# Loading both MLP weights behind the last V of a decode attention kernel, with the MLP features interleaved over the partitions

## The chip, the cores and the metric

The kernel runs on one core of one Trainium2 chip. The metric is the device time of one launch in microseconds (us). Times are quoted as the median of the runs of one kernel.

## The reference

One query token, 32 heads, 32768 cached keys of 128 features each, then an MLP with 1376 hidden features.

```python
x = A_x                                             # [1, 1, 512], bf16
q = (layernorm(x) @ wq)                             # 32 heads x 128
scores = q . k_cache * 128 ** -0.5                  # k_cache [1, 32, 32768, 128]
o = softmax(scores) @ v_cache                       # v_cache of the same shape
h = x + o @ wo
z = layernorm(h) @ w1 + b1                          # w1 [512, 1376], b1 [1376]
act = z * tanh(softplus(z))                         # Mish
out = h + act @ w2                                  # w2 [1376, 512]
```

The two caches are 512 MiB of bf16. Everything else is small: w1 and w2 are 1.4 MB each, b1 is 2.75 KB.

Of the kernel before, what the change touches and what calls it, by code (L numbers as in the profile page):

```python
# [6 lines left out]
BF16 = mybir.dt.bfloat16  # L7
F32 = mybir.dt.float32
I32 = mybir.dt.int32
ALU = mybir.AluOpType  # L10
# [3 lines left out]
PE, ACT, DVE, POOL, SP = "pe", "act", "dve", "pool", "sp"  # L14
# [5 lines left out]
LAST_K = [128, 32, 32, 32, 32]  # L20
LAST_V = [32, 32, 32, 32, 64, 32, 16, 8, 8]

W1A = 5
W2A = 6

LAG = 8

# [2 lines left out]
PRIV = "_p"  # L30
# [172 lines left out]
def build_kernel(nc, A_x, A_k_cache, A_v_cache, A_wq, A_wo, B_w1, B_b1, B_w2, out, NE=4):  # L203
# [3 lines left out]
    H = HD // Dh  # L207
    Sk = A_k_cache.shape[2]
    F = B_w1.shape[1]
    assert D == 512  # L210
    KC = D // 128
    R = 8
    GH = Sk // (128 * R)
    NCOL = GH * R
    NK = H * GH
    FJ = (F + 127) // 128
    FLAST = F - (FJ - 1) * 128
    SC = 1.0 / math.sqrt(Dh)
    EPS = 1e-5
    NH0 = min(4, H)  # L220
# [4 lines left out]
    def sb(shape, dt, name):  # L225
        cm = nc.sbuf_tensor(name, shape, dt)
        t = cm.__enter__()
        allocs.append(cm)
        return t.ap()
# [10 lines left out]
    w1v = sb([128, KC, F], BF16, "w1_sb")  # L240
    w2v = sb([128, FJ, D], BF16, "w2_sb")
# [4 lines left out]
    identb = sb([128, 128], BF16, "identb")  # L246
# [10 lines left out]
    xcT = sb([128, KC], BF16, "xcT")  # L257
# [14 lines left out]
    yrs = sb([128, D], F32, "yrs")  # L272
    ycol = sb([128, KC], F32, "ycol")
    pscr = sb([1, 2], F32, "pscr")
    FP = FJ + FJ % 2
    b1r = sb([FP, 128], BF16, "b1r")
    b1T = sb([128, FJ], F32, "b1T")
    hs = sb([128, 8, FJ], F32, "hs")
    actT = sb([128, FJ], BF16, "actT")
# [2 lines left out]
    MEANX, SSQ, LNV, RSTD, EPSC, SSQ2, LNV2, RSTD2, MEANH = (lnb[:, 16 + i:17 + i] for i in range(9))  # L282

    S_b = ps([128, 512], "sps")
# [4 lines left out]
    T_b = [ps([128, R * 128], f"tps{i}", BF16) for i in range(2)]  # L289
# [6 lines left out]
    YC = yps[:, 0:KC]  # L296
    HROW = 128
    YM = yps[:, 256:257]
    pre = S_b

    loads = plan_loads(H, GH)
    kload, vload = {}, {}
# [5 lines left out]
    wqa = ring[:, wq_at:wq_at + KC * NH0 * Dh].rearrange("p (kc n) -> p kc n", kc=KC)  # L308
    wqb = ring[:, wq_at + KC * NH0 * Dh:wq_at + KC * HD].rearrange("p (kc n) -> p kc n", kc=KC) if H > NH0 else None
# [8 lines left out]

    sem = nc.alloc_semaphore
    sems = {e: sem(f"ev_{e}") for e in (PE, ACT, DVE, POOL, SP)}  # L320
    for c in (ACT + PRIV, DVE + "0" + PRIV, DVE + "1" + PRIV, PE + "0" + PRIV, PE + "1" + PRIV, "x", "xr", "b1", "wqa", "wqb", "wo", "w1a", "w1b", "w2a", "w2b", "w2c", "out"):
        sems[c] = sem(f"s_{c}")
    for ld in loads:
        if ld.chan not in sems:
# [16 lines left out]
    def program(S):  # L341
        t_ = nc.tensor
        a = nc.scalar
        v = nc.vector
        g_ = nc.gpsimd
        sp = nc.sync
# [12 lines left out]
        def load_weights(which):  # L359
            if which == "wqa":  # L360
                S.dma(SP, lambda: sp.dma_start(  # L361
                    wqa, A_wq[:, 0:NH0 * Dh].rearrange("(p kc) n -> p kc n", kc=KC)).then_inc(sems["wqa"], 16))
            elif which == "wqb" and H > NH0:
                S.dma(SP, lambda: sp.dma_start(
                    wqb, A_wq[:, NH0 * Dh:HD].rearrange("(p kc) n -> p kc n", kc=KC)).then_inc(sems["wqb"], 16))
            elif which == "wo":
                S.dma(SP, lambda: sp.dma_start(
                    wo_sb[:, :, :], A_wo.rearrange("(h k) n -> k h n", k=128)).then_inc(sems["wo"], 16))
            elif which == "w12":
                S.dma(SP, lambda: sp.dma_start(  # L370
                    w1v[:, :, 0:W1A * 128],
                    B_w1.rearrange("(kc p) f -> p kc f", p=128)[:, :, 0:W1A * 128]).then_inc(sems["w1a"], 16))
            elif which == "late":
                S.dma(SP, lambda: sp.dma_start(
                    w1v[:, :, W1A * 128:F],
                    B_w1.rearrange("(kc p) f -> p kc f", p=128)[:, :, W1A * 128:F]).then_inc(sems["w1b"], 16))
                for a_, b_, s_ in ((0, W2A, "w2a"), (W2A, FJ - 1, "w2b")):
                    S.dma(SP, lambda a_=a_, b_=b_, s_=s_: sp.dma_start(
                        w2v[:, a_:b_, :],
                        B_w2[a_ * 128:b_ * 128, :].rearrange("(j p) n -> p j n", p=128)).then_inc(sems[s_], 16))  # L380
                S.dma(SP, lambda: sp.dma_start(
                    w2v[0:FLAST, FJ - 1, :], B_w2[(FJ - 1) * 128:F, :]).then_inc(sems["w2c"], 16))

        S.dma(SP, lambda: sp.dma_start(xTb[:, :], A_x[0, 0, :].rearrange("(p kc) -> p kc", kc=KC)).then_inc(sems["x"], 16))
        order = [(ld.pos, ld) for ld in loads]
        order += [(-1.0, "wqa"), (GH - 0.5, "wqb"), (GH + 2 * LAG + 0.2, "wo"), (2 * GH + 2 * LAG + 0.2, "w12"), (1e9, "late")]
        for _, ld in sorted(order, key=lambda o: o[0]):
            if isinstance(ld, str):
                load_weights(ld)
            else:  # L390
                issue(ld)
        S.dma(SP, lambda: sp.dma_start(out[0, 0, :].rearrange("(g n) -> g n", g=4), outsb[0:128:32, :]).then_inc(sems["out"], 16),
              waits=["fin"])
        S.wait(SP, [("out", 16)])

        for x in range(NX):
# [5 lines left out]
        S.step(POOL, lambda: g_.memset(b1r[:, :], 0.0), name="b1z")  # L402
        S.dma(POOL, lambda: g_.dma_start(xrow[0:1, :], A_x[0:1, 0, :]).then_inc(sems["xr"], 16))
        S.dma(POOL, lambda: g_.dma_start(
            b1r[0:FJ - 1, :], B_b1[0:(FJ - 1) * 128].rearrange("(j m) -> j m", m=128)).then_inc(sems["b1"], 16), waits=["b1z"])
        S.dma(POOL, lambda: g_.dma_start(
            b1r[FJ - 1:FJ, 0:FLAST], B_b1[(FJ - 1) * 128:F].rearrange("(o m) -> o m", o=1)).then_inc(sems["b1"], 16))
        for k, done in (("k", f"kf{NK - GH - 1}"), ("v", f"pv{NK - 2 * GH - 1}")):
            for x in range(NX):
                S.dma(POOL, lambda x=x, k=k: g_.sem_inc(sems[f"{k}x{x}"], -16), waits=[done])  # L410
# [5 lines left out]
        S.step(DVE, lambda: v.memset(oneb[0:1, :], 1.0))  # L416
        S.step(DVE, lambda: v.memset(onesf[:, :], 1.0))
        S.step(DVE, lambda: v.memset(qT[:, H:H + 1], 0.0))
        S.step(DVE, lambda: v.memset(yps[:, :], 0.0), name="consts")


# [10 lines left out]
               name="ident", waits=["iota"])  # L432
# [213 lines left out]
        for t in range(GH):  # L646
            group(H, t)
            if t == LAG + 5:
                S.step(DVE, lambda: v.tensor_reduce(ysum[:, :], yrow[:, :], AXX, ALU.add), name="ysum",
                       waits=[f"yr{hl - 1}"])  # L650
                S.step(DVE, lambda: v.tensor_scalar_mul(MEANH, ysum[:, :], 1.0 / D), name="meanh", waits=["ysum"])

                for c in range(KC):
                    S.step(DVE, lambda c=c: v.tensor_tensor(
                        yrs[:, c * 128:(c + 1) * 128], yrow[:, c * 128:(c + 1) * 128], ident[:, :], ALU.mult),
                        waits=[f"yr{hl - 1}"], name=(f"yrs" if c == KC - 1 else None))
                S.step(DVE, lambda: v.tensor_reduce(
                    ycol[:, :], yrs[:, :].rearrange("p (c n) -> p c n", c=KC), AXX, ALU.add), name="ycol", waits=["yrs"])
            if t == LAG + 9:
                S.step(PE, lambda: t_.matmul(YC, ident[:, :], ycol[:, :], start=True, stop=False,  # L660
                                             skip_group_check=True), waits=["ycol"])
                S.step(PE, lambda: t_.matmul(T_b[0][:, 0:FP], b1r[:, :], identb[0:FP, 0:FP],
                                             is_transpose=True, start=True, stop=True),
                       name="b1t", waits=[("b1", 32), f"ev{NK - 2}", f"ev{NK - 1}"])
                S.step(DVE, lambda: v.tensor_copy(b1T[:, :], T_b[0][:, 0:FJ]), name="b1T", waits=["b1t"])
        for t in range(LAG):
            group(H + 1, t)

# [3 lines left out]
            name="oT", waits=[f"pv{NK - 1}", f"o1s{hl}"])  # L672
        y_cols(hl)
        for s in range(2):
            S.step(PE, lambda s=s: t_.matmul(
                YM, wbh[:, s:s + 1].to_broadcast([128, 128]), oT[:, :],
                start=False, stop=(s == 1), skip_group_check=True),
                waits=(["wbh"] if s == 0 else ()), name=("ym" if s == 1 else None))
        S.step(DVE, lambda: v.tensor_scalar(HC, YC, YM, MEANH, ALU.subtract, ALU.subtract),
               name="hc", waits=["ym"])  # L680
# [1 line left out]
        S.step(DVE, lambda: v.tensor_tensor(SQ, HC, HC, ALU.mult), name="sq2", waits=["hc"])  # L682
        S.step(DVE, lambda: v.tensor_reduce(SSQ2, SQ, AXX, ALU.add), name="ssq2", waits=["sq2"])
        S.step(DVE, lambda: v.tensor_copy(hcol[:, :], YC), name="hcol")
        for j in range(FJ):
            W = 128 if j < FJ - 1 else FLAST
            for kc in range(KC):
                S.step(PE, lambda j=j, W=W, kc=kc: t_.matmul(  # L688
                    pre[0:W, j:j + 1], w1v[:, kc, j * 128:j * 128 + W], xcT[:, kc:kc + 1],
                    start=(kc == 0), stop=(kc == KC - 1)),  # L690
                    name=("hid" if j == FJ - 1 and kc == KC - 1 else None),
                    waits=(["xcT", ("w1a", 16), f"exq{H - 1}"] if j == 0 and kc == 0
                           else [("w1b", 16)] if j == W1A and kc == 0 else ()))
            if j == FJ // 2:
                S.step(PE, lambda: t_.matmul(V_REG, onesm[:, :], SSQ2, start=True, stop=True), name="v2",
                       waits=["ssq2"])
        S.step(ACT, lambda: a.activation(LNV2, V_REG, ACTF.Ln, bias=EPSC), name="ln2", waits=["v2"])
        S.step(ACT, lambda: a.activation(RSTD2, LNV2, ACTF.Exp, scale=-0.5), name="rstd2", waits=["ln2"])
        for c in range(KC):
            S.step(PE, lambda c=c: t_.matmul(  # L700
                yps[32 * c:32 * c + 1, HROW:HROW + 128], hcol[:, c:c + 1], ident[:, :],
                start=False, stop=False, skip_group_check=True), waits=(["hcol"] if c == 0 else ()))
        z, zm, e, u, uz, den, rden = (hs[:, k, :] for k in range(7))
        S.step(DVE, lambda: v.scalar_tensor_tensor(z, pre[:, 0:FJ], RSTD2, b1T[:, :], ALU.mult, ALU.add),
               name="z", waits=["hid", "rstd2", "b1T"])
        S.step(DVE, lambda: v.tensor_scalar_min(zm, z, 30.0), name="zm", waits=["z"])
        S.step(ACT, lambda: a.activation(e, zm, ACTF.Exp), name="e", waits=["zm"])
# [5 lines left out]
        for j in range(FJ):  # L713
            W = 128 if j < FJ - 1 else FLAST
            waits = ["act"] if j == 0 else []
            if j in (0, W2A, FJ - 1):
                waits.append(({0: "w2a", W2A: "w2b"}.get(j, "w2c"), 16))
            for c in range(KC):
                S.step(PE, lambda j=j, W=W, c=c: t_.matmul(  # L719
                    yps[32 * c:32 * c + 1, HROW:HROW + 128], actT[0:W, j:j + 1], w2v[0:W, j, c * 128:(c + 1) * 128],  # L720
                    start=False, stop=(j == FJ - 1), skip_group_check=True),
# [47 lines left out]
```

## The kernel before: what the change touches

The SP queue issues all large loads in one order: wq, then K and V by pieces of 4 MB (the first K and the last V in smaller pieces), with wo and the first 640 of the 1376 columns of w1 slipped in early. The rest of w1, and w2, follow the last V.

```python
elif which == "w12":                      # early, in the third head
    w1v[:, :, 0:W1A * 128] <- B_w1.rearrange("(kc p) f -> p kc f", p=128)[:, :, 0:W1A * 128]   # 1280 B rows
elif which == "late":                     # after the last V
    w1v[:, :, W1A * 128:F] <- B_w1...[:, :, W1A * 128:F]                                       # 1472 B rows
    for a_, b_, s_ in ((0, W2A, "w2a"), (W2A, FJ - 1, "w2b")):
        w2v[:, a_:b_, :] <- B_w2[a_ * 128:b_ * 128, :].rearrange("(j p) n -> p j n", p=128)    # 1024 B rows
    w2v[0:FLAST, FJ - 1, :] <- B_w2[(FJ - 1) * 128:F, :]
# ... (each is one sp.dma_start with its own semaphore; condensed here)

# POOL's queue, at the start of the kernel: b1 as 10 rows of 256 B and a rest of 192 B
b1r[0:FJ - 1, :] <- B_b1[0:(FJ - 1) * 128].rearrange("(j m) -> j m", m=128)
b1r[FJ - 1:FJ, 0:FLAST] <- B_b1[(FJ - 1) * 128:F].rearrange("(o m) -> o m", o=1)
# ... (turned into columns b1T by one PE transpose while PE waits for V)

# the tail, after the last V: feature f = 128 j + p sits in partition p, column j
for j in range(FJ):                       # FJ = 11
    W = 128 if j < FJ - 1 else FLAST      # FLAST = 96
    for kc in range(KC):                  # KC = 4
        matmul(pre[0:W, j:j + 1], w1v[:, kc, j * 128:j * 128 + W], xcT[:, kc:kc + 1], ...)
# ... z, Mish -> actT
for j in range(FJ):
    for c in range(KC):
        matmul(yps[32 * c:32 * c + 1, HROW:HROW + 128], actT[0:W, j:j + 1], w2v[0:W, j, c * 128:(c + 1) * 128], ...)
```

(Assignments with an arrow stand for DMA starts.) In a w1 matmul the w1 block is the stationary operand, so it is what the weight load reads: the trace of the kernel before lists 44 weight loads of it, 40 of 128x128 and 4 of 128x96.

## Time and profile before

| | before |
|---|---|
| time, median of 6 runs | 1288.78 us (1288.39 to 1289.03) |
| span of the profiled run | 1286.6 us |
| DMA engines | 9 tenths or more busy in 39 of 40 slices, 426 GB/s |
| last V landed | 1277.35 us |
| last weights landed | 1283.31 us |
| output copy starts | 1284.18 us |

Two lines of the page of the kernel before; the digits are busy tenths in 40 equal slices of the span, and GB/s is what the DMA engines moved in each slice.

```profile
DMA  9999999999999999999999999999999999999998
GB/s 375 424 409 426 428 435 428 436 428 435 428 435 429 434 430 432 431 433 431 433 431 432 430 434 430 433 430 434 430 431 433 431 433 431 433 430 433 431 419 324
```

The load stream never drains (9 tenths in 39 of 40 slices): the kernel is DMA bound until the last V has landed at 1277.35. What follows is a tail of about 9 us in which a chain of small operations runs on three engines. The chain that ended last, in order of time (start us, length us, what), kernel before:

```profile
1257.87 19.49 DMA ring<-in_A_v_cache_dram
1277.35 0.04 issue
1277.40 0.41 PE ops L530 x8
...
1278.79 0.17 DVE xcT L681
1278.96 0.07 DVE lnb L682
1279.03 0.92 PE sps L688 x24
1279.95 0.43 PE hlp L695 x2
1280.38 0.76 PE sps L688 x20
...
1282.55 0.18 DVE actT L712
1282.74 0.04 issue
1282.78 1.37 PE yps L719 x44
1284.15 0.02 issue
1284.18 0.29 DVE outsb L723
```

The 44 w1 matmuls are the two rows with `sps L688`: 24 take 0.92 us, 38 ns each. The 44 w2 matmuls are `yps L719`. No DMA appears after 1277.35, so the tail is bound by computing; the weights arrive just in time. Their loads, from the page's list of DMA issues (KB each, median us from issue to landing); the 640 KB one is the early part of w1:

```profile
w_sb<-in_B_w_dram SPq DMA_DIRECT2D x1, 768.0 KB, 23.1
w_sb<-in_B_w_dram SPq DMA_DIRECT2D x1, 736.0 KB, 21.4
w_sb<-in_B_w_dram SPq DMA_DIRECT2D x1, 640.0 KB, 24.0
...
w_sb<-in_B_w_dram SPq DMA_DIRECT2D x1, 512.0 KB, 15.1
w_sb<-in_B_w_dram SPq DMA_DIRECT2D x1, 96.0 KB, 14.7
```

For each load the trace has 16 increments of its semaphore, and the time of each. I read them as one from each of the 16 DMA engines, though the trace does not name the engine. For the last V they run from 1272.05 to 1277.35 us: on this reading the slowest engine is 5.3 us behind the fastest. The wait is over only with the last increment: PE goes on at 1277.40.

### The profile page before, as it was taken

The numbers are of one execution on the slowest core, as the hardware profiler recorded it, in microseconds if no ns is written. First come the engines' busy times: TensorE is split into PE (matmuls) and PEld (weight loads), VectorE is DVE, ScalarE is ACT, GpSimd is POOL, SyncE is SP. The second block draws the span as 40 slices with busy tenths as digits, with TensorE's granted clock in tenths as the row PEclk, the third lists the DMA queues.
The fourth block names the chain that finished last, engine by engine and source line by source line (L and its number), as shares of the span: only waits on it lengthen the run. The fifth ranks groups of instructions, "written<-read, shape, count | busy, mean of one in ns | idle before, by whom it ended". The sixth has DMA issues, their size and how long they took to land.

```text
span 1286.6 us, 52403 instructions
## 1 busy us (share of the span) xinstructions
PE 1027.5 (80%) x25072; PEld 994.2 (77%) x25103; DVE 759.4 (59%) x1353; ACT 34.0 (3%) x134; POOL 2.7 (0%) x12
## 2 busy tenths in 40 slices
PE   6858787788787788788888778888877887877886
PEld 6747787788787787777887777877777877777885
DVE  5635565566565565665666655655655655656663
ACT  0000000000000000000000000000000000000000
POOL 0000000000000000000000000000000000000000
PEclk8878989988899988988989988989989989989996
DMA  9999999999999999999999999999999999999998
GB/s 375 424 409 426 428 435 428 436 428 435 428 435 429 434 430 432 431 433 431 433 431 432 430 434 430 433 430 434 430 431 433 431 433 431 433 430 433 431 419 324
DMA packets 28800, 548.45 MB, mean 426 GB/s; under 512 B 2696, under 2 KB 9704, under 8 KB 10984
## 3 DMA queue, kind: packets, MB, share of 16 engines
q1 hardware_dynamic: 28680, 548.09, 99.7%
q8 instruction: 20, 0.33, 0.1%
q14 instruction: 4, 0.03, 0.0%
q0 software_dynamic: 96, 0.00, 0.0%
HBM read 548.08 MB, written 0.00 MB: 426 GB/s over the span
## 4 chain that ended last, share of the span: by engine, by line
DMA 57%; PE 38%; DVE 3%; issue 1%; SPq 0%; ACT 0%
DMA ring<-in_A_k_cache_dram 56%; PE tps L477 20%; PE sps L500 8%; PE ops L530 8%; DVE kt L488 2%; DMA ring<-in_A_v_cache_dram 2%; PE hlp L599 1%; DVE scb L580 1%; PE hlp L582 1%; DVE pmax L578 1%; PE hlp L587 1%; SPq L357 0%; PE sps L688 0%; PE yps L719 0%; SPq L361 0%
## 5 line engine op out<-in xcount | busy, mean ns | idle before, releaser
L488 DVE COPY kt<-tps 128x1024 bf16<-128x1024 bf16 x1024 | 707.8, 692 | 494.0 <-PE tps L477 486.9
L477 PE MATMUL tps<-identb,ring 128*128 128x128 bf16 x8192 | 693.7, 234 | 179.4 <-DMA ring<-in_A_k_cache_dram 176.1
L477 PEld LDWEIGHTS tps<-identb,ring 128*128 128x128 bf16 x8192 | 523.8, 104 | 188.4 <-DMA ring<-in_A_k_cache_dram 182.6
L530 PE MATMUL ops<-pbuf,ring 128*128 128x32 bf16 x8192 | 361.7, 178 | 57.2 <-DMA ring<-in_A_v_cache_dram 55.7
L500 PE MATMUL sps<-qcur,kt 128*128 128x32 bf16 x8192 | 376.0, 180 | 11.0 <-DVE scb L580 7.1
L500 PEld LDWEIGHTS sps<-qcur,kt 128*128 128x128 bf16 x8192 | 328.6, 99 | 18.7 <-DVE scb L580 14.4
L530 PEld LDWEIGHTS ops<-pbuf,ring 128*128 128x128 bf16 x8192 | 281.6, 97 | 70.1 <-DMA ring<-in_A_v_cache_dram 59.1
L590 ACT ACTIVATE pbuf<-scb,nbias 128x192 bf16<-128x192 f32 x32 | 14.6, 455 | 1164.8 <-PE ops L530 1094.8
L599 PE MATMUL hlp<-esum,onesf 128*128 128x1 f32 x128 | 18.6, 249 | 0.1
L599 PEld LDWEIGHTS hlp<-esum,onesf 128*128 128x128 f32 x128 | 16.8, 190 | 0.0
L578 DVE TENSOR_REDUCE pmax<-sps 128x1 f32<-128x256 f32 x32 | 13.3, 415 | 0.5 <-PE sps L500 0.5
L580 DVE COPY scb<-sps 128x256 f32<-128x256 f32 x32 | 13.3, 415 | 0.0
L582 PE MATMUL hlp<-ident,pmax 128*1 128x128 f32 x64 | 13.1, 289 | 0.1
L594 ACT ACTIVATE pbuf<-scb,nbias 128x64 bf16<-128x64 f32 x32 | 11.1, 348 | 60.2 <-PE ops L530 60.2
L587 PE MATMUL hlp<-gmax,onesr 1*128 1x1 f32 x64 | 12.1, 256 | 0.1
L617 DVE TENSOR_SCALAR o1s<-ops,rtot 128x1 f32<-128x1 f32 x32 | 6.7, 210 | 8.0 <-PE ops L530 8.0
L587 PEld LDWEIGHTS hlp<-gmax,onesr 1*128 1x128 f32 x64 | 9.4, 182 | 1.2 <-DVE gmax L585 0.2
L607 DVE COPY qcur<-qT 128x1 bf16 (+1 forms) x63 | 9.3, 147 | 0.0
L585 DVE TENSOR_REDUCE gmax<-hlp 1x1 f32<-1x128 f32 x32 | 8.6, 270 | 0.2
L621 DVE SCALAR_TENSOR_TENSOR ocur<-ops,rtot,o1s 128x1 bf16<-128x1 f32 x31 | 6.6, 213 | 0.7 <-PE ops L530 0.7
L443 PE MATMUL hlp<-xnT,ring 128*128 128x1 bf16 x128 | 3.7, 164 | 3.1 <-issue 3.1
L443 PEld LDWEIGHTS hlp<-xnT,ring 128*128 128x128 bf16 x128 | 3.6, 99 | 3.2 <-issue 3.2
(85 smaller groups left out, 55.2 us busy)
## 6 DMA issues: line engine op xcount, KB each, us to landing
ring<-in_A_k_cache_dram SPq DMA_DIRECT2D x62, 4096.0 KB, 22.6
ring<-in_A_v_cache_dram SPq DMA_DIRECT2D x61, 4096.0 KB, 20.8
ring<-in_A_v_cache_dram SPq DMA_DIRECT2D x9, 1024.0 KB, 19.8
ring<-in_A_k_cache_dram SPq DMA_DIRECT2D x5, 1024.0 KB, 15.5
wo_sb<-in_A_wo_dram SPq DMA_DIRECT2D x1, 4096.0 KB, 36.8
ring<-in_A_wq_dram SPq DMA_DIRECT2D x1, 3584.0 KB, 30.4
ring<-in_A_k_cache_dram SPq DMA_DIRECT2D x1, 2048.0 KB, 12.1
ring<-in_A_v_cache_dram SPq DMA_DIRECT2D x1, 2048.0 KB, 21.2
```

The lines of the kernel that those rows point to most:

```text
L477: S.step(PE, lambda r=r: t_.matmul(tb[:, r * 128:(r + 1) * 128], block("k", i, r), identb[:, :], is_transpose=True, start=True, stop=True) ...
L488: dve(i, lambda: v.tensor_copy(kt[:, i % NE, :], T_b[i % 2][:, :]), f"ev{i}", waits)
L500: S.step(PE, lambda r=r, c=c: t_.matmul(S_b[:, c:c + WIDE], kt[:, i % NE, r * 128:(r + 1) * 128], q.to_broadcast([128, WIDE]), start=True, ...
L530: S.step(PE, lambda r=r, c=c: t_.matmul(ob[:, 0:WIDE], block("v", i, r), pbuf[:, c:c + 1].to_broadcast([128, WIDE]), start=(r == 0 and g i ...
L578: dve(i, lambda: v.tensor_reduce(pmax[:, :], S_b[:, 0:NCOL], AXX, ALU.max), f"pmax{hs}", [f"qkb{hs}"])
L580: dve(i, lambda: v.tensor_copy(scb[:, :], S_b[:, 0:NCOL]), f"sc{hs}", [])
L582: S.step(PE, lambda: t_.matmul(A_REG, pmax[:, :], ident[:, :], start=True, stop=True), name=f"A{hs}", waits=[f"pmax{hs}"] + (["qT" if H > ...
L587: S.step(PE, lambda: t_.matmul(B_REG, onesr[0:1, :], gmax[0:1, :], start=True, stop=True), name=f"B{hs}", waits=[f"gmax{hs}"], priv=pe_cha ...
L590: S.step(ACT, lambda: a.activation(pbuf[:, 0:CV], scb[:, 0:CV], ACTF.Exp, bias=nb[:, :], scale=SC, accum_out=esum[:, 0:1]), name=f"exp{hs} ...
L594: S.step(ACT, lambda: a.activation(pbuf[:, CV:NCOL], scb[:, CV:NCOL], ACTF.Exp, bias=nb[:, :], scale=SC, accum_out=esum[:, 1:2]), name=f"e ...
L599: S.step(PE, lambda s=s: t_.matmul(C_REG, onesf[:, :], esum[:, s:s + 1], start=(s == 0), stop=(s == 1)), name=(f"C{hs}" if s else None), w ...
L607: S.step(DVE, lambda j=j, n=n: v.tensor_copy(qcur[:, j:j + 1], qT[:, n:n + 1] if S.round is None else qT[:, bass.ds(S.round + (3 - j), 1)] ...
```

## The change

The intent is to take the 640 KB of w1 out of the stream in front of the last V, and to make up for the longer load behind it with longer rows: w1 in four quarters of 2752 B rows, w2 with ten consecutive rows per partition (5120 B in each of two pieces). For w2 to be laid out like this, feature f = 10 p + j has to sit in partition p, column j. So the w1 weight loads read every tenth column, b1 is loaded 10 values per partition, and the transpose of b1 goes away.

```diff
-            elif which == "w12":
-                S.dma(SP, lambda: sp.dma_start(
-                    w1v[:, :, 0:W1A * 128], ...).then_inc(sems["w1a"], 16))
             elif which == "late":
-                S.dma(SP, lambda: sp.dma_start(
-                    w1v[:, :, W1A * 128:F], ...).then_inc(sems["w1b"], 16))
+                for kc in range(KC):
+                    S.dma(SP, lambda kc=kc: sp.dma_start(
+                        w1v[:, kc, :], B_w1[kc * 128:(kc + 1) * 128, :]).then_inc(sems[f"w1_{kc}"], 16))
                 for a_, b_, s_ in ((0, W2A, "w2a"), (W2A, FJ - 1, "w2b")):
                     S.dma(SP, lambda a_=a_, b_=b_, s_=s_: sp.dma_start(
                         w2v[:, a_:b_, :],
-                        B_w2[a_ * 128:b_ * 128, :].rearrange("(j p) n -> p j n", p=128)).then_inc(sems[s_], 16))
+                        B_w2[0:FM, :].rearrange("(p j) n -> p j n", j=FJ - 1)[:, a_:b_, :]).then_inc(sems[s_], 16))
 ...
-            b1r[0:FJ - 1, :], B_b1[0:(FJ - 1) * 128].rearrange("(j m) -> j m", m=128)) ...
+            b1r[:, 0:FJ - 1], B_b1[0:FM].rearrange("(p j) -> p j", j=FJ - 1)) ...
-            b1r[FJ - 1:FJ, 0:FLAST], B_b1[(FJ - 1) * 128:F].rearrange("(o m) -> o m", o=1)) ...
+            b1r[0:FLAST, FJ - 1:FJ], B_b1[FM:F].rearrange("(p o) -> p o", o=1)) ...
 ...
-        for j in range(FJ):
-            W = 128 if j < FJ - 1 else FLAST
-            for kc in range(KC):
+        for kc in range(KC):
+            for j in range(FJ):
+                W = 128 if j < FJ - 1 else FLAST
                 S.step(PE, lambda j=j, W=W, kc=kc: t_.matmul(
-                    pre[0:W, j:j + 1], w1v[:, kc, j * 128:j * 128 + W], xcT[:, kc:kc + 1],
-                    start=(kc == 0), stop=(kc == KC - 1)),
+                    pre[0:W, j:j + 1], w1v[:, kc, j:FM:FJ - 1] if j < FJ - 1 else w1v[:, kc, FM:F], xcT[:, kc:kc + 1],
+                    start=False, stop=(kc == KC - 1), skip_group_check=True),
```

(Cut: the names of semaphores, W2A from 6 to 5, a zeroed accumulator for the w1 sums.) The last 96 values of b1 are now 96 elements of 2 B, one per partition.

More of the change, by code (lines that the diff above doesn't have):

```diff
@@ L21 @@
 LAST_V = [32, 32, 32, 32, 64, 32, 16, 8, 8]
-W1A = 5
-W2A = 6
+W2A = 5
 LAG = 8
@@ L216, in build_kernel @@
     FJ = (F + 127) // 128
-    FLAST = F - (FJ - 1) * 128
+    FM = (FJ - 1) * 128
+    FLAST = F - FM
     SC = 1.0 / math.sqrt(Dh)
@@ L274, in build_kernel @@
     pscr = sb([1, 2], F32, "pscr")
-    FP = FJ + FJ % 2
-    b1r = sb([FP, 128], BF16, "b1r")
+    b1r = sb([128, FJ], BF16, "b1r")
     b1T = sb([128, FJ], F32, "b1T")
@@ L298, in build_kernel @@
     YM = yps[:, 256:257]
-    pre = S_b
+    pre = S_b[:, 320:320 + FJ]
     loads = plan_loads(H, GH)
@@ L320, in build_kernel @@
     sems = {e: sem(f"ev_{e}") for e in (PE, ACT, DVE, POOL, SP)}
-    for c in (ACT + PRIV, DVE + "0" + PRIV, DVE + "1" + PRIV, PE + "0" + PRIV, PE + "1" + PRIV, "x", "xr", "b1", "wqa", "wqb", "wo", "w1a", "w1b", "w2a", "w2b", "w2c", "out"):
+    for c in (ACT + PRIV, DVE + "0" + PRIV, DVE + "1" + PRIV, PE + "0" + PRIV, PE + "1" + PRIV, "x", "xr", "b1", "wqa", "wqb", "wo", "w1_0", "w1_1", "w1_2", "w1_3", "w2a", "w2b", "w2c", "out"):
         sems[c] = sem(f"s_{c}")
@@ L368, in load_weights @@
                     wo_sb[:, :, :], A_wo.rearrange("(h k) n -> k h n", k=128)).then_inc(sems["wo"], 16))
-            elif which == "w12":
-                S.dma(SP, lambda: sp.dma_start(
-                    w1v[:, :, 0:W1A * 128],
-                    B_w1.rearrange("(kc p) f -> p kc f", p=128)[:, :, 0:W1A * 128]).then_inc(sems["w1a"], 16))
             elif which == "late":
-                S.dma(SP, lambda: sp.dma_start(
-                    w1v[:, :, W1A * 128:F],
-                    B_w1.rearrange("(kc p) f -> p kc f", p=128)[:, :, W1A * 128:F]).then_inc(sems["w1b"], 16))
+                for kc in range(KC):
+                    S.dma(SP, lambda kc=kc: sp.dma_start(
+                        w1v[:, kc, :], B_w1[kc * 128:(kc + 1) * 128, :]).then_inc(sems[f"w1_{kc}"], 16))
                 for a_, b_, s_ in ((0, W2A, "w2a"), (W2A, FJ - 1, "w2b")):
@@ L379, in load_weights @@
                         w2v[:, a_:b_, :],
-                        B_w2[a_ * 128:b_ * 128, :].rearrange("(j p) n -> p j n", p=128)).then_inc(sems[s_], 16))
+                        B_w2[0:FM, :].rearrange("(p j) n -> p j n", j=FJ - 1)[:, a_:b_, :]).then_inc(sems[s_], 16))
                 S.dma(SP, lambda: sp.dma_start(
-                    w2v[0:FLAST, FJ - 1, :], B_w2[(FJ - 1) * 128:F, :]).then_inc(sems["w2c"], 16))
+                    w2v[0:FLAST, FJ - 1, :], B_w2[FM:F, :]).then_inc(sems["w2c"], 16))
         S.dma(SP, lambda: sp.dma_start(xTb[:, :], A_x[0, 0, :].rearrange("(p kc) -> p kc", kc=KC)).then_inc(sems["x"], 16))
         order = [(ld.pos, ld) for ld in loads]
-        order += [(-1.0, "wqa"), (GH - 0.5, "wqb"), (GH + 2 * LAG + 0.2, "wo"), (2 * GH + 2 * LAG + 0.2, "w12"), (1e9, "late")]
+        order += [(-1.0, "wqa"), (GH - 0.5, "wqb"), (GH + 2 * LAG + 0.2, "wo"), (1e9, "late")]
         for _, ld in sorted(order, key=lambda o: o[0]):
@@ L404, in program @@
         S.dma(POOL, lambda: g_.dma_start(
-            b1r[0:FJ - 1, :], B_b1[0:(FJ - 1) * 128].rearrange("(j m) -> j m", m=128)).then_inc(sems["b1"], 16), waits=["b1z"])
+            b1r[:, 0:FJ - 1], B_b1[0:FM].rearrange("(p j) -> p j", j=FJ - 1)).then_inc(sems["b1"], 16), waits=["b1z"])
         S.dma(POOL, lambda: g_.dma_start(
-            b1r[FJ - 1:FJ, 0:FLAST], B_b1[(FJ - 1) * 128:F].rearrange("(o m) -> o m", o=1)).then_inc(sems["b1"], 16))
+            b1r[0:FLAST, FJ - 1:FJ], B_b1[FM:F].rearrange("(p o) -> p o", o=1)).then_inc(sems["b1"], 16))
         for k, done in (("k", f"kf{NK - GH - 1}"), ("v", f"pv{NK - 2 * GH - 1}")):
@@ L418, in program @@
         S.step(DVE, lambda: v.memset(qT[:, H:H + 1], 0.0))
+        S.step(DVE, lambda: v.memset(pre, 0.0))
         S.step(DVE, lambda: v.memset(yps[:, :], 0.0), name="consts")
@@ L661, in program @@
                                              skip_group_check=True), waits=["ycol"])
-                S.step(PE, lambda: t_.matmul(T_b[0][:, 0:FP], b1r[:, :], identb[0:FP, 0:FP],
-                                             is_transpose=True, start=True, stop=True),
-                       name="b1t", waits=[("b1", 32), f"ev{NK - 2}", f"ev{NK - 1}"])
-                S.step(DVE, lambda: v.tensor_copy(b1T[:, :], T_b[0][:, 0:FJ]), name="b1T", waits=["b1t"])
+                S.step(DVE, lambda: v.tensor_copy(b1T[:, :], b1r[:, :]), name="b1T", waits=[("b1", 32)])
         for t in range(LAG):
@@ L684, in program @@
         S.step(DVE, lambda: v.tensor_copy(hcol[:, :], YC), name="hcol")
-        for j in range(FJ):
-            W = 128 if j < FJ - 1 else FLAST
-            for kc in range(KC):
+        for kc in range(KC):
+            for j in range(FJ):
+                W = 128 if j < FJ - 1 else FLAST
                 S.step(PE, lambda j=j, W=W, kc=kc: t_.matmul(
-                    pre[0:W, j:j + 1], w1v[:, kc, j * 128:j * 128 + W], xcT[:, kc:kc + 1],
-                    start=(kc == 0), stop=(kc == KC - 1)),
+                    pre[0:W, j:j + 1], w1v[:, kc, j:FM:FJ - 1] if j < FJ - 1 else w1v[:, kc, FM:F], xcT[:, kc:kc + 1],
+                    start=False, stop=(kc == KC - 1), skip_group_check=True),
                     name=("hid" if j == FJ - 1 and kc == KC - 1 else None),
-                    waits=(["xcT", ("w1a", 16), f"exq{H - 1}"] if j == 0 and kc == 0
-                           else [("w1b", 16)] if j == W1A and kc == 0 else ()))
-            if j == FJ // 2:
+                    waits=(["xcT"] if kc == 0 else []) + [(f"w1_{kc}", 16)] if j == 0 else ())
+            if kc == 1:
                 S.step(PE, lambda: t_.matmul(V_REG, onesm[:, :], SSQ2, start=True, stop=True), name="v2",
@@ L703, in program @@
         z, zm, e, u, uz, den, rden = (hs[:, k, :] for k in range(7))
-        S.step(DVE, lambda: v.scalar_tensor_tensor(z, pre[:, 0:FJ], RSTD2, b1T[:, :], ALU.mult, ALU.add),
+        S.step(DVE, lambda: v.scalar_tensor_tensor(z, pre, RSTD2, b1T[:, :], ALU.mult, ALU.add),
                name="z", waits=["hid", "rstd2", "b1T"])
```

## The prediction

> **What bounds the kernel now.** The load stream. The page's slices show the 16 DMA engines at 9 tenths in 39 of 40 slices; the SP queue's share is 99.7% and the rate 426 GB/s. Only less DMA time before the last V lands, or a shorter tail after it, can shorten the 1286.6 us span.
>
> **The tail (chain of waits, timeline, issues to landing).** The last V lands at 1277.35. Then PV, oT, wo and xcT reach 1278.96; the 44 w1 matmuls and the fp32 variance matmul end near 1281.1; the Mish chain ends at 1282.74; the 44 w2 matmuls take 1.37 us; the output copy starts at 1284.18. The weights land at 1279.64 (second half of w1), 1281.81, 1283.08 and 1283.31 (w2), just ahead of their use: no DMA wait in the tail. The slowest engine sets a landing: the last V's 16 increments spread over 5.3 us.
>
> **Removed from the stream.** The first w1 load (640 KB near 113-118 us) is 32 packets of 1280 B per engine, 55 ns each in the packet records: 1.76 us of every engine. As the stream never drains, the last V should land 1.7 us earlier, near 1275.6. The b1 load becomes 224 descriptors of 2 to 20 B instead of 17 of 12 to 256 B; recorded small ones take 9 to 18 ns: I charge 0.15 us.
>
> **Added behind the last V.** Packet times by size: 1024 B 46 ns, 1472 B 62, 2048 B 85, 4096 B 160, 8192 B 312, so about 9 ns plus 37 ns per KB. [...] Estimates: 108 ns for a 2752 B row of w1 and 195 ns for 5120 B of w2. Per engine: w1 32 x 108 = 3.5 us (was 3.74), w2 16 x 195 + 6 x 46 = 3.4 us (was 3.96). So all loads end about 0.8 us earlier than 1283.31. Estimated landings: w1 quarters 1276.6, 1277.5, 1278.4, 1279.2; w2 1280.8, 1282.4, 1282.65.
>
> **The new tail.** xcT at 1277.3. w1 matmuls now go quarter by quarter, the last waiting for 1279.2, then 11 at 37 ns (24 took 0.92 us): hidden done near 1279.8. Mish 1.65 us: 1281.4. Twenty w2 matmuls, then a wait for 1282.4, then 24 more: done near 1283.3 against 1284.15. Gain 0.8 to 0.9 us. The tail turns from compute bound to weight-load bound.
>
> **The risk.** w1's columns are now read with a step of 10 elements (20 B). [...] no strided weight load is in this trace. At 60 ns each little is lost[...]. Expected: 1288.0 us, range 1286.6 to 1289.6.
>
> Off the path: the dropped b1 transpose (0.19 us, while PE waits for V).
>
> **What would show it.** V's last landing 1.5 to 1.8 us earlier from the end of its own stream; DMA waits newly listed for the w1 and w2 matmuls; packets of 2752 B near 108 ns and 5120 B near 195 ns[...].
>
> **What would make it wrong.** A strided weight load above 70 ns; spread of the engines changing by a microsecond; b1's small descriptors delaying the first K.

The sum that the forecast makes: the last V 1.7 us earlier puts xcT at 1277.3, the waits for the weights take back about half of that, and the kernel ends 0.8 to 0.9 us sooner, 1288.8 less 0.8 being the 1288.0 expected. The 60 and 70 ns are what-ifs, not measured costs.

## More of the kernel before

The three groups of experiments ran on three chips (numbers 5, 14 and 0; the record does not name the chip of the first measurement), and there is one trace per kernel; that of the kernel before is from the first measurement. A comparison of traces across groups is therefore also one across chips.

Below, "mean" and "slowest" of a load are the mean and the last of its 16 increments.

## The result, and the profile after

| | before | after |
|---|---|---|
| time, median of 6 runs each | 1288.78 us | 1288.98 us (1288.71 to 1289.31) |
| ratio of the runs | | 1.0002 (0.9989 to 1.0015) |
| span of the profiled run | 1286.6 | 1287.4 |
| fourth K load: mean of 16 increments / slowest | 10.64 / 11.18 | 11.52 / 13.87 |
| last V: mean of 16 increments / slowest | 1274.66 / 1277.35 | 1273.73 / 1277.04 |
| xcT to end of the w1 matmuls | 2.2 us | 3.3 us |
| last weights landed | 1283.31 | 1283.87 |
| output copy starts | 1284.18 | 1284.98 |

A ratio is the mean time of one kernel's runs over that of the other's of the same rounds, so it is not quite the ratio of the medians quoted. The prediction's range holds the time, but 0.8 us of gain was expected in it and none came.

The chain that ended last, kernel after:

```profile
1257.61 19.43 DMA ring<-in_A_v_cache_dram
1277.04 0.05 issue
1277.09 0.41 PE ops L527 x8
...
1278.48 0.17 DVE xcT L675
1278.65 0.07 DVE lnb L676
1278.72 1.48 PE sps L682 x22
1280.21 0.43 PE hlp L688 x2
1280.63 1.31 PE sps L682 x22
...
1283.36 0.18 DVE actT L705
1283.54 0.04 issue
1283.59 1.37 PE yps L712 x37
1284.96 0.02 issue
1284.98 0.29 DVE outsb L716
```

Two things differ. The last V landed only 0.31 us earlier, not 1.7. And 22 w1 matmuls now take 1.48 us, 67 ns each, where 24 took 0.92. (`x37` for 44 w2 matmuls is a gap in the records.) The chain names no weight DMA: with w1 this slow, this run's tail is again bound by computing. The issues of the large weight loads after:

```profile
w_sb<-in_B_w_dram SPq DMA_DIRECT2D x4, 344.0 KB, 20.1
w_sb<-in_B_w_dram SPq DMA_DIRECT2D x2, 640.0 KB, 16.6
```

Where did the early V go? It was lost in the first 11 us. Busy time of each engine and, in the last two columns, the DMA share and GB/s, in stretches from 6 us on. First the kernel before, then the kernel after:

```profile
6.00:8.00 2.00, 1.98 (x27) 2.00 (x28) 0.00 (x0) 0.00 (x0) 0.00 (x0) 1.00 1.02 368
8.00:10.00 2.00, 0.81 (x17) 0.75 (x15) 1.57 (x5) 0.00 (x0) 0.00 (x0) 1.00 0.97 377
```

```profile
6.00:8.00 2.00, 1.84 (x22) 1.87 (x22) 0.00 (x0) 0.00 (x0) 0.00 (x0) 1.00 0.98 254
8.00:10.00 2.00, 0.43 (x17) 0.34 (x13) 1.50 (x5) 0.00 (x0) 0.00 (x0) 1.00 0.72 283
```

The engines moved 254 and 283 GB/s in place of 368 and 377. In 6 to 8 us their share was still 0.98, but packets took longer: of the 8 KB packets of the fourth K load, nine took 0.88 to 1.52 us, where the median of that size in the whole run is 0.31 and the longest of this load in the kernel before 0.66. (These figures are from the packet records; a packet counts in the stretch in which it starts.) In 8 to 10 us the share fell to 0.72, and the packet records have 13.7 packets in flight on average, where the kernel before has 16.0. That is when the new b1 loads run (their last increment comes at 10.57 us, before at 8.14). The short first K loads land late: the fourth K load is 0.9 us late by the mean and 2.7 us by the slowest.

### The profile page after: what moved, and what is told of

Same layout as the page of the kernel before. It is cut to its first block, busy times and chain, and to the rows that moved or that the text cites. A ratio compares the mean times of both kernels' runs of the same rounds, so it can differ in the third digit from the quotient of the medians.

```text
span 1287.4 us, 52435 instructions
## 1 busy us (share of the span) xinstructions
PE 1032.2 (80%) x25102; PEld 996.9 (77%) x25102; DVE 759.2 (59%) x1354; ACT 34.0 (3%) x134; POOL 2.6 (0%) x12
## 4 chain that ended last, share of the span: by engine, by line
DMA 58%; PE 38%; DVE 3%; issue 0%; SPq 0%; ACT 0%
DMA ring<-in_A_k_cache_dram 54%; PE tps L474 20%; PE ops L527 7%; PE sps L497 7%; DMA ring<-in_A_v_cache_dram 4%; DVE kt L485 2%; PE hlp L596 1%; DVE scb L577 1%; PE hlp L579 1%; DVE pmax L575 1%; PE hlp L584 1%; PE yrow L544 1%; PE sps L682 0%; SPq L356 0%; PE yps L712 0%
## 5 line engine op out<-in xcount | busy, mean ns | idle before, releaser
L544 PE MATMUL yrow<-wo_sb,ocur 128*128 (+1 forms) x31 | 11.7, 377 | 0.0
L599 DVE RECIPROCAL rtot<-hlp 128x1 f32<-128x1 f32 x32 | 5.4, 169 | 1.0 <-PE hlp L596 1.0
```

What stands on the lines that cost most here:

```text
L544: S.step(PE, lambda: t_.matmul(yrow[:, :], ocur[:, 0:1].to_broadcast([128, 128]), rhs, start=False, stop=(h == H - 2), skip_group_check=Tr ...
```

## The experiments

Twelve kernels ran, in three groups of four. "Mean difference" is the mean of the kernel's runs minus the mean of the kernel before's runs of the same rounds. The intervals of all ratios are about 0.13% to each side (1.7 us) and all contain 1, so no run here is a proven speed-up of the whole kernel; what the trace shows inside is far sharper. The runs of a kernel scatter by 0.3 us (standard deviation) in most cases, by 1.0 in after_again and 0.6 in contig_wrong.

| kernel | 4th K load: mean / slowest | last V: mean / slowest | median us | mean difference us |
|---|---|---|---|---|
| before | 10.64 / 11.18 | 1274.66 / 1277.35 | 1288.4 to 1288.8 | |
| after (first measurement) | 11.52 / 13.87 | 1273.73 / 1277.04 | 1288.98 | +0.28 |
| after_again | 11.24 / 13.01 | 1273.33 / 1275.92 | 1289.16 | +0.87 |
| contig_wrong | 11.60 / 13.17 | 1274.00 / 1277.46 | 1289.60 | +0.98 |
| no20 | 10.79 / 12.51 | 1272.92 / 1275.96 | 1288.79 | +0.29 |
| before_small | 10.93 / 11.57 | 1274.98 / 1278.02 | 1289.14 | +0.45 |
| late_only | 10.79 / 11.05 | 1273.03 / 1275.91 | 1288.34 | -0.27 |
| b1row | 10.65 / 11.04 | 1272.91 / 1276.07 | 1288.16 | -0.57 |
| no2 | 10.67 / 11.20 | 1272.84 / 1275.40 | 1287.82 | -0.71 |
| b1late | 10.57 / 10.98 | 1272.89 / 1275.61 | 1288.03 | -0.44 |
| step5 | 10.74 / 11.55 | 1273.15 / 1276.15 | 1287.85 | -0.75 |
| step2 | 10.66 / 11.23 | 1272.88 / 1275.73 | 1287.77 | -0.75 |
| step1 | 10.52 / 11.16 | 1272.76 / 1275.40 | 1288.13 | -0.34 |
| best2 | 10.42 / 11.33 | 1272.78 / 1275.41 | 1288.10 | -0.35 |

The first theory (A) was that the b1 loads throw the DMA-bound stream back by 2.7 us for good. Its rival (R1) was that an early loss is made up again by slack in the stream. The second (B) was that the step of the w1 weight loads costs what the tail grew by; its rival (R2) that the order by quarters or the granted clock does.

### late_only: only the early part of w1 moves

```diff
-(2 * GH + 2 * LAG + 0.2, "w12")
+(1e9 - 1.0, "w12")
```

> The kernel before with the first w1 load alone moved behind the last V, all layouts as before. Theory A says the stream is DMA bound, so the last V lands 1.7 to 2.0 us earlier, near 1275.5; but the weights then still end near 1283.3, and the w2 matmuls wait for the last of them, so the kernel gains only 0.2 to 0.6 us (1288.2 to 1288.6). Rival R1: the last V does not move and the time grows by about 0.5 us or more, as the weights land later.

The last V landed at 1275.91 (slowest) and 1273.03 (mean): 1.44 and 1.63 us earlier than before. The gain of the whole kernel was small, a mean difference of -0.27 us, as expected, but not for the reason expected. In the chain that ended last, the wait is not for w2 (landed by 1283.21, without a wait) but for the rest of w1, behind its moved part, whose landing hardly moved (1279.60, before 1279.64):

```profile
1257.79 21.81 DMA w_sb<-in_B_w_dram
1279.60 0.05 issue
1279.64 0.26 PE sps L688 x4
```

From there the rest of the tail ran as before and the last w2 matmuls still ended near 1284.1. So the first half of the idea works as it was costed: 640 KB out of the stream are worth about 1.6 us at the last V. What is behind the V then sets the end.

### b1row: b1 loaded as one row

```diff
-            b1r[:, 0:FJ - 1], B_b1[0:FM].rearrange("(p j) -> p j", j=FJ - 1)) ...
-            b1r[0:FLAST, FJ - 1:FJ], B_b1[FM:F].rearrange("(p o) -> p o", o=1)) ...
+            b1r[0:1, :], B_b1[0:F].rearrange("(o m) -> o m", o=1)) ...
+                for j in range(FJ):      # while PE waits for V
+                    matmul(S_b[0:W, 336 + j:337 + j], b1r[0:1, j:FM:FJ - 1], oneb[0:1, 0:1], start=True, stop=True)
```

(Cut: b1r as one row, its cleared accumulator and the semaphore counts.)

> The changed kernel with b1 loaded as one row of 1376 elements (16 pieces of 172 B) and turned into columns by 11 one-row matmuls while PE waits for V. Theory A (the 224 tiny b1 descriptors hold the first K loads up by about 2.7 us, and the DMA-bound stream never gets that back): the third K load lands near 8.7 us instead of 11.35, the last V near 1274.5 instead of 1277.04, and the kernel takes 2 to 2.8 us less than the changed one, near 1286.4. Rival R1 (the stream has slack or jitter, so an earlier start is lost again and the last V lands where the ring lets it): the last V stays within 0.7 us of 1277.0 and the time near 1289.0.

The start is cured: the fourth K load is back at 10.65 / 11.04 us. The last V is 0.97 us earlier than in the changed kernel (slowest) and 0.82 us by the mean, and the kernel is about 0.8 us faster than the changed one by the medians. Both theories miss. Theory A is right about the cause and wrong about the size (2 to 2.8 us was expected); R1 is wrong, since what the engines lost on average stays lost. (By the slowest increment alone it would be less clear: in after_again, below, the changed kernel's last V came at 1275.92, a little before b1row's 1276.07.)

The size has a simple reading. The mean of the changed kernel's 16 increments was 0.87 us behind b1row's at the fourth K load, 0.97 at 193 us, 0.84 at 971 us and 0.82 at the last V. The other traces agree, each against b1row (fourth K load, then last V): after_again 0.59 and 0.42, contig_wrong 0.95 and 1.09, and all kernels with b1 as a row, without the 2 B loads or with them later within 0.25 both times. So the mean loss is carried through the whole stream. The slowest increment was 2.8 us late at the fourth K load and 0.97 us late at the last V. An engine that was thrown back early need not be one of those that are last 1270 us later. The trace does not tell which engine an increment came from, so this last step is argued from the two series, not shown.

### before_small: the kernel before plus the tiny b1 loads

```diff
+        S.dma(POOL, lambda: g_.dma_start(
+            b1d[:, 0:FJ - 1], B_b1[0:1280].rearrange("(p j) -> p j", j=FJ - 1)).then_inc(sems["b1d"], 16))
+        S.dma(POOL, lambda: g_.dma_start(
+            b1d[0:FLAST, FJ - 1:FJ], B_b1[1280:F].rearrange("(p o) -> p o", o=1)).then_inc(sems["b1d"], 16))
```

> The kernel before plus the two tiny b1 loads of the change (128 x 20 B and 96 x 2 B) into a tile that nobody reads. Theory A: every load from the third K on lands 2 to 3 us later, the last V near 1280, and the kernel takes 2 to 2.8 us more than before, near 1291.3. Rival R1: no load beyond the first few is late, time within 0.4 us of before.

The kernel took 0.45 us more and the last V came 0.67 us later (slowest), so the tiny loads do cost. But the fourth K load was only 0.3 us late by the mean, not 0.9, and the last V 0.3 us by the mean too. Here they stand behind the ordinary b1 loads and are issued 1 us later, at 3.55 and 4.11 us in place of 2.52 and 3.09. The cost therefore seems to depend on when they run and what they run beside, which the last group takes up.

### contig_wrong: consecutive columns, wrong on purpose

```diff
-                    pre[0:W, j:j + 1], w1v[:, kc, j:FM:FJ - 1] if j < FJ - 1 else w1v[:, kc, FM:F], xcT[:, kc:kc + 1],
+                    pre[0:W, j:j + 1], w1v[:, kc, j * 128:j * 128 + W] if j < FJ - 1 else w1v[:, kc, FM:F], xcT[:, kc:kc + 1],
```

> The changed kernel with the w1 weight loads reading 128 consecutive columns in place of every tenth one; nothing else differs, and the result is wrong on purpose. Theory B (the step of 20 B makes each w1 weight load 68 instead of 37 ns and that lies on the tail's path): 22 matmuls take 0.8 us instead of 1.5, the last quarter now waits for its load, and the kernel takes 0.7 to 1.1 us less than the changed one, near 1288.1. Rival R2 (the order by quarters or the throttled clock slows them, not the step): spacing stays near 68 ns and the time near 1289.0.

The spacing did what theory B said: 22 matmuls in 0.86 us, 39 ns each, with the order by quarters kept. The granted clock was 0.50 in the w1 stretch of the trace of before (38 ns each) as in that of after (67 ns), so R2 is out. The time did not: 1289.60, slower than the changed kernel. The end of this run's chain shows why nothing was gained.

```profile
1270.30 13.89 DMA w_sb<-in_B_w_dram
1284.19 0.04 issue
1284.23 0.84 PE yps L712 x24
```

With w1 fast again, the tail hangs on the second half of w2, which landed at 1284.19; 24 matmuls follow it whatever came before. The step is worth at most the difference between the two limits: in the changed kernel's own trace w2b landed at 1283.71, so the 24 matmuls of 0.84 us would have ended near 1284.6 where they ended at 1284.96. That is 0.4 us, not the 1.1 us by which the w1 part grew. The same sum gives 0.4 us in b1row and 0.1 us in b1late; it is worked out from the landings, and no run measured it by itself.

### after_again: the changed kernel as a control

> The changed kernel itself again, as the control on this chip for the consecutive-columns run, which came out slower (1289.6) where theory B wanted it faster. If that was the chip or the stream's luck: the changed kernel lands anywhere from 1288.8 to 1289.8 here, and the mean of the 16 landings of the fourth K load is again 0.8 to 1.0 us behind the kernel before (10.64). If reading consecutive columns truly costs time, it stays at 1288.9 to 1289.1 with small scatter.

It came out at 1289.16 with runs from 1288.39 to 1290.77. So contig_wrong is not slower than the changed kernel; the changed kernel itself scatters more than the one before (1288.06 to 1289.37 in the same rounds). The mean of the fourth K load was again late, 11.24 us, below the 11.44 that 0.8 us would have made. Its last V came at 1275.92 (slowest) and 1273.33 (mean), 1.43 and 1.33 us earlier than before, so in this trace most of the early V was kept. The gain was lost behind it: the tail waited 0.9 us for w2b, which landed at 1284.06, so here the loads were the limit. The traces of before and after each show three packets of 16 KB on the instruction queue after 1262 us, of 1.03 to 1.10 us, one of them near 1281. If such a packet holds up the slowest engine, the landing is late by about as much. That is one candidate for the scatter; no run tested it.

### step5, step2, step1: how much does the step cost?

All three have b1 as a row. Features are interleaved in blocks of 128 x JB: JB = 5 keeps w2 in 5120 B rows, JB = 2 gives 2048 B rows, JB = 1 the old 1024 B rows. The w1 columns are read with a step of JB.

```diff
+    JB = 5            # 2, 1
+    def FEAT(j):
+        b, i = divmod(j, JB)
+        return slice(b * 128 * JB + i, (b + 1) * 128 * JB, JB)     # last 96 features: consecutive
-    w1v[:, kc, j:FM:FJ - 1] if j < FJ - 1 else w1v[:, kc, FM:F]
+    w1v[:, kc, FEAT(j)]
```

(Cut: w2's loads by blocks; b1 as in b1row.) The pair theory of these texts is that any step other than 1 costs as much as a step of 10. A second theory stood against it, by which the cost grows with the step. Of step5's forecast under it the time is left.

> b1 as a row, and the MLP features interleaved in two blocks of 640 (feature 640 b + 5 p + i), so w2 still comes in 5120 B rows but w1 is read with a step of 5 elements (10 B). [...] Pair theory [...]: 68 ns as with a step of 10. [...] the w2 loads then end the tail: 1287.7 to 1288.1.

> b1 as a row, features interleaved in pairs (feature 256 b + 2 p + i): w1 read with a step of 2 elements (4 B), w2 in 2048 B rows. [...] Pair theory: 68 ns. w2 takes 85 ns per 2 KB row, so its loads end about 0.25 us later than with 5120 B rows: 1287.9 to 1288.4.

> b1 as a row and no interleaving: w1 read in consecutive columns, w2 in 1024 B rows of 46 ns, all else as changed. Spacing 37 ns; the w2 loads end about 0.5 us later than with 5120 B rows and bound the tail: 1288.1 to 1288.6. If the descriptor size were worth nothing, it would be the fastest of the three.

Weight loads of the w1 block, from the view of the tile (minimum, median and maximum ns of one, start of the first and the last, forms), in the order before (step 1), after (step 10), step5, step2:

```profile
L688 PEld LDWEIGHTS sps<-xcT,w_sb x44: 104/104/291, 1279.0 to 1280.8; 128*128 128x128 bf16 x40, 128*96 128x96 bf16 x4
```

```profile
L682 PEld LDWEIGHTS sps<-xcT,w_sb x44: 137/157/304, 1278.7 to 1281.6; 128*128 128x128 bf16 x40, 128*96 128x96 bf16 x4
```

```profile
L699 PEld LDWEIGHTS sps<-xcT,w_sb x44: 117/131/291, 1277.8 to 1280.1; 128*128 128x128 bf16 x40, 128*96 128x96 bf16 x4
```

```profile
L699 PEld LDWEIGHTS sps<-xcT,w_sb x44: 104/104/191, 1277.4 to 1279.5; 128*128 128x128 bf16 x40, 128*96 128x96 bf16 x4
```

One weight load takes 104 ns with a step of 1 or 2, 131 with 5 and 157 with 10; loads overlap, and 22 matmuls take 0.86, 0.85, 1.11 and 1.50 us, so 39, 39, 50 and 68 ns each. (That is the stretch over the count. The median from one start to the next is 27, 27, 40 and 58 ns; the differences are about the same.) So a step of 4 B (2 elements) costs nothing over consecutive columns, 10 B (5 elements) costs 11 ns a matmul, 20 B (10 elements) costs 29 ns. The pair theory is out, as a step of 2 is free here. In these three steps the cost grows with the step; what makes it, no run shows.

In time, step5 and step2 both came 0.75 us below the kernel before, and in those rounds the slowest step5 run (1287.97) was below the fastest of before (1288.06). step1 gained 0.34. In step2 the second half of w2 ends the tail:

```profile
1269.38 13.09 DMA w_sb<-in_B_w_dram
1282.47 0.04 issue
1282.51 0.94 PE yps L730 x28
```

All three times lie in or just below what was expected; step2 was expected a little behind step5 and is level with it.

### no2, no20: which of the two b1 loads?

no2 leaves the 96 loads of 2 B out, no20 the 128 rows of 20 B; b1 is then partly zero. Their outputs are wrong, which doesn't matter for the times.

```diff
 no2:
-        S.dma(POOL, lambda: g_.dma_start(
-            b1r[0:FLAST, FJ - 1:FJ], B_b1[FM:F].rearrange("(p o) -> p o", o=1)).then_inc(sems["b1"], 16))
 no20:
-        S.dma(POOL, lambda: g_.dma_start(
-            b1r[:, 0:FJ - 1], B_b1[0:FM].rearrange("(p j) -> p j", j=FJ - 1)).then_inc(sems["b1"], 16), waits=["b1z"])
```

(Cut: the semaphore's count, and in no20 the wait for b1z on the load that is left.)

> The changed kernel without the 96 loads of 2 B (the last 96 values of b1 stay 0, so the result is slightly wrong on purpose). If the 2 B elements hold the engines up, the mean of the 16 landings of the fourth K load falls from 11.2 to 11.6 back to about 10.6 and the kernel takes 1288.0 to 1288.4. If it is the 20 B rows, it stays above 11.2 and the time near 1289.

> The changed kernel without the 128 rows of 20 B (1280 values of b1 stay 0, wrong on purpose), with the 2 B loads kept. Mirror of the run without the 2 B loads: if the 2 B elements do it, the fourth K load's mean landing stays at 11.2 or later and the time near 1289; if the 20 B rows do it, 10.6 and 1288.2.

Without the 2 B loads the start is clean (10.67 / 11.20) and the kernel takes 1287.82. Without the 20 B rows the slowest engine of the fourth K load is still 1.3 us late (12.51) and the kernel takes 1288.79. So the loss does not come without the 2 B loads. But they do not make it alone: in no20 the mean of the fourth K load was 10.79, only 0.15 us late and not above 11.2 as forecast, and the last V (1272.92 / 1275.96) came as early as b1row's. The longer time of no20 is therefore not explained by the start of the stream; in its trace the second half of w2 landed at 1283.35, 0.4 us after no2's, and why is open. The long 8 KB packets at the start tell the same: over 0.7 us there are nine in after, six each in after_again and contig_wrong, and none in before, b1row, no2, no20 or b1late. In these runs the mean loss came only with both loads. Whether it needs the two together, or the 2 B loads at the later moment at which they run behind the others (issued at 3.09 us, in no20 at 2.50), no run tells apart.

### b1late: the same tiny loads, 480 us later

```diff
-            ... waits=["b1z"])
+            ... waits=["b1z", f"kf{12 * GH}"])
```

> The changed kernel with its two tiny b1 loads issued some 480 us into the stream in place of the start. If they cost engine time wherever they run, the fourth K load is back at 10.6 but the landings step up by 0.5 to 1 us near 480 us and the kernel stays near 1289.0. If they only collide with the short loads at the start, there is no such step and the time is that of b1 as a row, 1288.0 to 1288.4.

Issued in the middle of the stream, the same 224 elements cost almost nothing. The lag of b1late's landings behind those of b1row, by the mean of the increments, goes from -0.11 us (loads that landed from 400 to 490 us) to +0.01 us (500 to 600 us), a step of 0.1 us, and the time is 1288.03. The start of b1late moves data again, in the same stretches as above:

```profile
6.00:8.00 2.00, 2.00 (x24) 1.73 (x24) 0.00 (x0) 0.00 (x0) 0.00 (x0) 1.00 0.86 337
8.00:10.00 2.00, 0.81 (x20) 0.76 (x17) 1.55 (x5) 0.00 (x0) 0.00 (x0) 1.00 1.04 420
```

So it is not the tiny loads by themselves that cost 0.9 us on the mean of the engines, but the tiny loads at the start. That the short K loads beside them are what matters there is the likely reading; other things differ at the start too, and no run varied the K loads.

### best2: more pieces of w2

step2 with the 96-row rest of w2 first and w2 in three pieces of 4, 4 and 2 blocks.

```diff
-                for a_, b_, s_ in ((0, 4, "w2a"), (4, 10, "w2b")):
+                # the rest (rows FM to F) first
+                for a_, b_, s_ in ((0, 4, "w2a"), (4, 8, "w2b"), (8, 10, "w2d")):
```

> A version to beat both: b1 as a row, features interleaved in pairs, and w2 in four pieces, the 96-row rest first and two blocks last, so that after the last landing 12 matmuls are left in place of 28. The last landing comes 0.1 to 0.2 us later than w2b's did, and 16 matmuls of 30 ns fewer follow: 1287.4 to 1287.8. If the order of pieces is worth nothing, 1287.8 as with pairs alone.

It took 1288.10, a mean difference of -0.35: it beats neither step2 nor step5. Only 12 matmuls were left after the last landing, as planned, but that landing came at 1283.08, 0.6 us after step2's w2b. By the mean of the increments the last load of each landed at the same time (1280.15, in step2 1280.11), so it was the slowest increment that came late, not the loads as a whole; why stays open.

## Why the prediction was right or wrong, point by point

- **"What bounds the kernel now."** Right: 640 KB less in the stream moved the last V (late_only), and a mean loss at its start came back at its end.
- **"the last V should land 1.7 us earlier".** Right for the move alone: late_only 1.44 us by the slowest engine, 1.63 by the mean. In the changed kernel 0.31 and 0.93 (1.43 and 1.33 in after_again, with a smaller loss at the start), because of the next point.
- **"recorded small ones take 9 to 18 ns: I charge 0.15 us".** This is the step that failed, a term of the sum that was mis-sized. The packets are as short as said (11 to 14 ns in the trace of after), but the K packets beside them took up to 1.52 us in place of 0.31, and then engines stood without a packet (13.7 packets in flight in place of 16.0). The cost was 0.8 to 0.9 us by the mean of the increments (changed kernel against b1row; 0.4 to 1.1 us over the three traces with these loads at the start), and about 0.8 us in the time. What stretches the K packets stays open. The prediction even listed "b1's small descriptors delaying the first K" among what would make it wrong; the trace of before could have warned only that b1 had no load of 2 B elements in it. Nor is size alone the cost: in b1late the same loads, amid 32 KB packets, put the landings back by 0.1 us.
- **"108 ns for a 2752 B row of w1 and 195 ns for 5120 B of w2".** Right: 109 and 196 ns in the records. The fit of 9 ns plus 37 ns per KB held for two sizes that were not in the first trace.
- **"all loads end about 0.8 us earlier", at 1282.65.** Right without the b1 stall: 1282.91 in b1row, 1282.71 in b1late. In the changed kernel 1283.87.
- **The strided weight load.** The risk was named, but what a step of 10 costs was not in the first trace, so the forecast had only what-ifs: at 60 ns little is lost, a load "above 70 ns" would make it wrong. It measured 68 ns, in place of 39 with consecutive columns. At 68 it cost an estimated 0.1 to 0.4 us in after, b1row and b1late, because the w1 matmuls, not the loads, then ended last.
- **"The tail turns from compute bound to weight-load bound."** Half right: bound by computing in the first trace of after, in b1row and in b1late, by the loads in after_again, contig_wrong, step5, step2, step1, best2, no2 and no20. Where the loads were the limit, the w2 matmuls waited 0.4 to 1.3 us for them in all; where computing was, the loads would have let them end 0.1 to 0.4 us sooner.
- **The sum.** Forecast -0.8 us; measured +0.2 by the medians. In the first trace of after the b1 term accounts for most of the difference (0.8 to 0.9) and the weight-load step for up to 0.4. In after_again's trace the b1 term is half of that, and a late w2b, whose cause is open, does most of the rest. The forecast range, 1286.6 to 1289.6, held only because it was wide enough for a gain of 2.2 us and a loss of 0.8: that the time lies in it is luck, not a sign that the sum was right.

## What to carry to other kernels

A layout that suits one large operand is paid for by the small ones that must follow it: here w2's rows asked for a strided weight load (68 ns a matmul in place of 39) and for a bias in 2 B pieces. Choose the smallest interleave that gives long enough rows (with b1 as a row, 2 and 5 took 1287.77 and 1287.85 us here, 10 took 1288.16), and load a bias as a row or keep it away from the short loads at the start (1288.16 and 1288.03 us here, against 1288.98). When 16 engines are far apart, read the mean as well as the slowest increment of a load: in these traces what the mean lost stayed lost (after against b1row 0.87 us at the fourth K load, 0.82 at the last V), and a late slowest engine did not always matter at the end (2.8 us late at the fourth K load, 0.97 at the last V).

## What these traces measured and leave open

- Element-sized loads beside others: 96 elements of 2 B and 128 rows of 20 B, whose packets take 11 to 14 ns, came with 8 KB packets of up to 1.52 us in place of 0.31 and put the fourth K load back by 0.9 us (mean) and 2.7 us (slowest) at the start; amid 32 KB packets they cost about 0.1 us.
- The spread of the 16 increments of one load in the bulk stream: in the kernel before it was 1.2 us at 9 us, 4.8 us at 198 us and 5.3 us at the last V. What makes it is open. It grew while most of the instruction packets of the next point ran (17 of about 1 us from 16 to 178 us, none as long from there to 1265 us); no run tested whether they are the cause.
- The kernel before has 20 packets of 16 KB on the instruction queue, about 1.05 us each, the last three between 1265 and 1282 us, beside the last V and the weights. What they cost the other loads, no run measured.
- The step of a weight load: bf16 matmuls of one column took 39 ns each at a step of 1 or 2 elements, 50 at 5 and 68 at 10. The granted clock was 0.50 in this stretch of the traces of before (step 1) and after (step 10).
